# Attention tiles that are read back by mirror: transposes two steps ahead, fetches in one list

## The chip, the cores and the metric

The kernel runs on one core of a Trainium2 chip. The time is that of one execution on the device in microseconds (us), of the slowest core, which here is the only one. Shown is the median of 3 runs. TensorE (PE in the rows) multiplies matrices, PEld is its weight load; VectorE (DVE), ScalarE (ACT) and GpSimd (POOL) do the work on elements; SyncE (SP) issues nearly all transfers.

## The reference

Attention without softmax, then an MLP, in float32:

```python
B, S, D = u.shape                       # 4, 3008, 256
scores = (1.0 / S) * np.matmul(z, z.transpose(0, 2, 1))    # z: 4 x 3008 x 64
attn = np.maximum(scores, 0.0) ** 2
x = (u * np.matmul(attn, v)).reshape(B * S, D)
h = x @ w_in                            # 256 -> 2048
g = h * np.clip(h + 3.0, 0.0, 6.0) / 6.0
return (g @ w_out).astype(np.float32)   # 2048 -> 256
```

The scores are a product of z with itself, so the matrix `attn` of a batch is symmetric.

## The kernel before

**Tiles.** A batch has 6 chunks c of queries (five of 512, the last of 448) and 12 pairs p of key blocks (two blocks of 128 keys). One step of the main loop (L546 to L602) is one pair of one chunk, 288 steps in all, g = 12 i + p, with i the chunk's number over all batches. In a step TensorE adds the pair's product with v to two accumulators `o` (`av`, 12 matmuls), and beside it runs units of the MLP of an earlier chunk: `up` (matmuls into `h`) and `down` (matmuls into `y`), 16 units a chunk. Each float32 operand is split into a high and a low part: `ah` and `al` of the attention, `gh` and `gl` of the MLP, `xh` and `xl` of its input. So each product takes three matmuls.

**New and mirrored pairs.** `scores` (L289) prepares the pair that is used one step later (two steps later for the first 28). Where the key block p // 2 is not below c, the pair is new: TensorE computes `s`, ACT and DVE make `rt`, its square `r2`, `ah` and `al`, and `keep` (L242) writes the square to DRAM in tiles `d` if a later chunk needs it. Where p // 2 < c, the pair is the mirror image of one computed before, and `from_mirror` (L259) makes it: chunk c has 2c such pairs, 30 a batch, 120 in all. `fetch_mirrored` (L226) reads such a tile `l` from `d` with four DMAs on SyncE's queue (two buffers of `l`). DVE then transposes it in two instructions into `rm` (L272), ACT casts `rm` to `ah` (L275) and DVE subtracts, `al` (L277):

```python
nc.vector.transpose(out=to, in_=of)                 # L272, twice: rm <- l
nc.scalar.copy(out=ah[:, :, :n], in_=rn)            # L275
nc.vector.tensor_tensor(out=al[:, :, :n], in0=rn, in1=f(ah[:, :, :n]), op=ALU.subtract)
```

**The MLP's chain.** After `up`, ACT makes `rt` from `h` (L396), DVE multiplies it (`rt`, L397), and later (`late`, run by `flush`) ACT casts `gh` (L80) and DVE subtracts `gl` (L81). `down` uses them. After the last `up` of a chunk, `urgent` makes this split run ahead of the next pair's `ah`.

**The chunk border.** When pair 11 is done, DVE multiplies each accumulator by `u` (`times_u`, L366). There is one buffer for each of the two `o`, so the next chunk's first matmul waits for this.

**What sets the order.** The instructions are issued in the order in which the code calls them; each engine works through its own in that order. In a step the loop calls `scores` for the pair ahead (L559), then fetches for the pairs up to two beyond it (L562), then loads and weight work, then `attend` (`av`, and `times_u` at the border), then the MLP's units. The tiles `rt`, `r2`, `rm` and raw weights share five buffers (`rpool`), the `ah` and `gh` share four (`apool`), and so do the `al` and `gl`.

Of the kernel before, what the change touches and what calls it, by code (L numbers as in the profile page):

```python
# [9 lines left out]
F32R = mybir.dt.float32r  # L10
# [5 lines left out]
P = 128  # L16
CH = 512
# [13 lines left out]
def relu2_attention_then_hswish_mlp(  # L31
# [30 lines left out]
    apool = ctx.enter_context(tc.tile_pool(name="apool", bufs=4))  # L62
# [9 lines left out]
    def f(ap):  # L72
        return ap.bitcast(F32)
# [19 lines left out]
    def flush_copies():  # L93
        while copies:
            copies.pop(0)()
# [72 lines left out]
    def fetch_v(b, p):  # L168

        if b == 0 and p < NPAIR - 1:  # L170
            raw = vpool.tile([P, 2, D], F32, tag="vl", name="vraw")
        else:
            raw = stg.tile([P, 2, D], F32, tag="stg", name="vraw")
        vh = vpool.tile([P, 2, D], F32R, tag="vh", name="vh")
        vt[b, p] = vh
        raws["v", p] = raw
        j0 = p * 2 * P
        for dst, queue in ((raw, nc.sync), (vh, nc.gpsimd))[:1 if b else 2]:
            if p < NPAIR - 1:
                queue.dma_start(  # L180
                    out=dst, in_=v[b, j0:j0 + 2 * P, :].rearrange("(r q) d -> q r d", q=P)
                )
            else:
                queue.dma_start(out=dst[:, 0, :], in_=v[b, j0:j0 + P, :])
                for h in range(2):
                    queue.dma_start(out=dst[64 * h:64 * h + 64, 1, :], in_=v[b, j0 + P:S, :])
# [7 lines left out]
    def fetch_z(b, k):  # L194
        if b == 0:
            raw = xpool.tile([P, CH], F32, tag=("xh0", "xh1", "xl0", "xl1")[k % 4], name="zraw")
        else:
            raw = stg.tile([P, CH], F32, tag="stg", name="zraw")
        zx = zpool.tile([P, CH], F32R, tag="zx", name="zx")
        zy = zpool.tile([P, CH], F32R, tag="zy", name="zy")  # L200
        zt[b, k] = (zx, zy)
        raws["z", k] = raw
        cols = slice(k * CH, (k + 1) * CH)
        nc.sync.dma_start(out=raw, in_=zz[b, :, cols])
        if b == 0 and k > 1:
            nc.gpsimd.dma_start(out=zx[0:64], in_=zz[b, 0:64, cols])
            nc.gpsimd.dma_start(out=zy[64:128], in_=zz[b, 64:128, cols])
# [11 lines left out]
    def flush():  # L219
        urgent.clear()  # L220
        while late:
            late.pop(0)()

    kept, mirrored = {}, {}

    def fetch_mirrored(b, c, p):  # L226


        if p // 2 >= c:
            return  # L230
        src = kept[b, p // 2, c]
        nk = width(c) // 32
        t = lpool.tile([P, 16, 64], F32, tag="l", name="l")
        for q in range(4):
            c0 = q * P + (p % 2) * 64
            nc.sync.dma_start(  # L236
                out=t[32 * q:32 * q + 32, :nk, :],
                in_=src[:, c0:c0 + 64].rearrange("(k e) f -> e k f", e=32),
            )
        mirrored[b, c, p] = t  # L240

    def keep(b, c, p, r2):  # L242

        k = p // 2
        if k <= c:
            return
        if p % 2 == 0:
            kept[b, c, k] = dpool.tile([width(k), CH], F32, tag=f"d{c}{k}", name=f"d{c}{k}")
        dst = kept[b, c, k]
        j0 = (p % 2) * 2 * P  # L250
        if p < NPAIR - 1:
            nc.sync.dma_start(
                out=dst[j0:j0 + 2 * P].rearrange("(r q) n -> q r n", q=P), in_=r2
            )
        else:
            nc.sync.dma_start(out=dst[j0:j0 + P], in_=r2[:, 0])
            nc.sync.dma_start(out=dst[j0 + P:j0 + P + 64], in_=r2[0:64, 1])

    def from_mirror(b, c, p):  # L259
        n = width(c)  # L260
        t = mirrored.pop((b, c, p))
        rn = rpool.tile([P, 2, CH], F32, tag="r", name="rm")[:, :, :n]
        ah = apool.tile([P, 2, CH], F32R, tag="ah", name="ah")
        al = apool.tile([P, 2, CH], F32R, tag="al", name="al")
        for r in range(2):
            if c < NCH - 1:
                to = rn[:, r].rearrange("p (q j e) -> p j q e", q=4, j=4)
                of = t.rearrange("p (j q) (r e) -> p r j q e", q=4, r=2)[:, r]
            else:
                to = rn[:, r].rearrange("p (k e) -> p k e", e=32)  # L270
                of = t[:, :n // 32, 32 * r:32 * r + 32]
            nc.vector.transpose(out=to, in_=of)  # L272
        if urgent:
            flush()
        nc.scalar.copy(out=ah[:, :, :n], in_=rn)  # L275
        flush_copies()
        nc.vector.tensor_tensor(  # L277
            out=al[:, :, :n], in0=rn, in1=f(ah[:, :, :n]), op=ALU.subtract
        )
        at[b, c, p] = (ah, al)  # L280
        flush()
# [7 lines left out]
    def scores(b, c, p, square_on_act=False):  # L289


        if p // 2 < c:
            return from_mirror(b, c, p)
# [38 lines left out]
    def width(c):  # L332
        return CH if c < NCH - 1 else S - CH * (NCH - 1)
# [98 lines left out]
    pairs = [(b, c, p) for b, c in chunks for p in range(NPAIR)]  # L432
# [62 lines left out]
    def weight_work(n):  # L495
        for _ in range(n):
            next(w_ops, None)
# [31 lines left out]
    with tc.manual_schedule():  # L529
        nc.vector.memset(three, 3.0)  # L530
        fetch_z(0, 0)
        fetch_v(0, 0)
        split_z(0, 0)
        fetch_z(0, 1)
        fetch_v(0, 1)
        weight_work(1)
        split_v(0, 0)
        split_z(0, 1)
        scores(0, 0, 0)
        fetch_z(0, 2)  # L540
        fetch_v(0, 2)
        scores(0, 0, 1)
        fetch_v(0, 3)
        g_done = 2
        g_fetched = 2
        for i, (b, c) in enumerate(chunks):  # L546
            ahead = b + 1 if c == NCH - 1 and b + 1 < B else None
            for p in range(NPAIR):
                g = i * NPAIR + p
                lead = 2 if g < FIRST else 1  # L550
                if i == 0:
                    if p + 1 < NPAIR:
                        split_v(0, p + 1)
                    if p % 2 == 0 and p // 2 + 2 < NCH:
                        split_z(0, p // 2 + 2)
                early = lead == 2 and p == NPAIR - 1
                if early:
                    attend(b, c, p)
                while g_done < min(g + lead + 1, len(pairs)):  # L559
                    scores(*pairs[g_done], square_on_act=i < 3)  # L560
                    g_done += 1
                while g_fetched < min(g_done + 2, len(pairs)):  # L562
                    fetch_mirrored(*pairs[g_fetched])
                    g_fetched += 1
                if i == 0:
                    if p + 4 < NPAIR:
                        fetch_v(0, p + 4)
                    if p % 2 == 0 and p // 2 + 3 < NCH:
                        fetch_z(0, p // 2 + 3)
                    if p == 6:  # L570
                        load_u(*chunks[0])
                        load_u(*chunks[1])
                maybe_split()
                if g >= FIRST:
                    weight_work(5)
                elif p < NPAIR - 2:
                    weight_work(4 if i else 2)
                if ahead and p < NPAIR - 1:
                    if p:
                        split_v(ahead, p - 1)  # L580
                    if p < NPAIR - 2:
                        fetch_v(ahead, p)
                    if p % 2 == 1:
                        fetch_z(ahead, p // 2)
                    elif p:
                        split_z(ahead, p // 2 - 1)
                elif b and c == 0 and p < 4:
                    if p in (1, 2):
                        split_v(b, NPAIR - 3 + p)
                    if p < 2:  # L590
                        fetch_v(b, NPAIR - 2 + p)
                    if p == 2:
                        fetch_z(b, NCH - 1)
                    if p == 3:
                        split_z(b, NCH - 1)
                if not early:
                    attend(b, c, p)
                if p == NPAIR - 1:
                    avs[0] += 1
                total = len(pairs) - FIRST  # L600
                target = max(0, g + 1 - FIRST) * ((len(chunks) - 1) * NU - 4) // total
                mlp_units(target - units_done[0])  # L602
        mlp_units(1)
        maybe_split()
        mlp_units(len(chunks) * NU - units_done[0])
# [46 lines left out]
```

## Time and profile before

| | |
|---|---|
| median of 3 runs | 2040.76 us (2036.39 to 2044.0) |
| the profiled execution | 2040.08 us |
| its span, from the first to the last instruction | 2038.3 us |
| granted TensorE clock, mean | 0.994 of full speed |
| TensorE matmuls busy | 1982.9 us, 97% |
| TensorE weight loads busy | 1634.6 us, 80% |
| VectorE busy | 1290.6 us, 63% |
| ScalarE busy | 989.7 us, 49% |
| DMA, mean | 87 GB/s |

How to read it: the busy time of an engine is the sum of its instructions' rows, and idle time is what lies between them. A row in order of time has the start, the duration, engine, line, operation, output and inputs, and in brackets how long the engine had idled before it and what ended that idling. Matmuls are pipelined: a row of one overlaps that of the next. A weight load stands a matmul or so ahead of the matmul that uses it.

### The profile page before, as it was taken

How to read it: one execution, taken by the hardware profiler on the slowest of the kernel's cores; microseconds unless marked ns; L12 is line 12 of the kernel's file. 1: busy time of each engine (PE TensorE's matmuls, PEld its weight loads, DVE VectorE, ACT ScalarE, POOL GpSimd, SP SyncE). 2: the span in 40 equal slices, each digit the busy share in tenths (PEclk: the TensorE clock that was granted, in tenths of full speed). 3: DMA queues.
4: the chain of work that ended last, by engine and by line, in shares of the span. 5: the costliest groups of instructions: out<-in, count | busy, mean ns of one | idle time of the engine just before them, and what ended most of it. 6: DMA issues, size and time to landing. Idle time of an engine off the chain costs nothing.

```text
span 2038.3 us, 22016 instructions
## 1 busy us (share of the span) xinstructions
PE 1982.9 (97%) x8688; PEld 1634.6 (80%) x8688; DVE 1290.6 (63%) x1397; ACT 989.7 (49%) x1057; POOL 14.2 (1%) x26
## 2 busy tenths in 40 slices
PE   8989999999999999999999999999999999999999
PEld 6767787888888877888888888788888887778888
DVE  7888666676556566667555666566756565556654
ACT  7754444465444444445545444444654544444444
POOL 2000000000000000000000000000000000000000
PEclk9999999999999999999999999999999999999999
DMA  9644151512222414252123141424222323232400
GB/s 298 194 112 121 53 111 47 129 56 104 70 88 53 111 32 111 56 131 78 71 70 102 42 116 34 101 60 118 86 93 60 100 46 107 52 91 51 101 19 20
DMA packets 313351, 178.14 MB, mean 87 GB/s; under 512 B 248480, under 2 KB 265888, under 8 KB 313248
## 3 DMA queue, kind: packets, MB, share of 16 engines
q1 hardware_dynamic: 309312, 172.54, 31.8%
q0 software_dynamic: 3936, 4.20, 0.9%
q8 instruction: 68, 1.11, 0.2%
q14 instruction: 35, 0.29, 0.0%
HBM read 104.07 MB, written 72.61 MB: 87 GB/s over the span
## 4 chain that ended last, share of the span: by engine, by line
PE 75%; DVE 10%; ACT 6%; DMA 5%; issue 3%; SPq 1%; POOL 0%; DVEq 0%; ACTq 0%; POOLq 0%
PE o L76 29%; PE h L76 20%; PE y L76 20%; PE s L76 7%; DVE rm L272 3%; DMA l<-d 2%; DVE al L277 2%; ACT ah L275 2%; DVE rt L397 1%; ACT rt L396 1%; DVE gl L81 1%; ACT gh L80 1%; SPq L236 1%; DMA vraw<-in_v_dram 1%; DMA vh<-in_v_dram 1%
## 5 line engine op out<-in xcount | busy, mean ns | idle before, releaser
L397 DVE SCALAR_TENSOR_TENSOR rt<-rt,h 128x1024 f32<-128x1024 f32 (+1 forms) x192 | 230.0, 1198 | 407.8 <-ACT rt L396 407.7
L76 PE MATMUL o<-ah,vl 128*128 128x512 f32 (+1 forms) x1152 | 450.3, 391 | 26.0 <-DVE u L366 20.0
L76 PE MATMUL o<-ah,vh 128*128 128x512 f32 (+1 forms) x1152 | 450.5, 391 | 0.0
L76 PE MATMUL o<-al,vh 128*128 128x512 f32 (+1 forms) x1104 | 435.9, 395 | 11.5 <-DVE al L277 9.9
L396 ACT ACTIVATE rt<-h,three 128x1024 f32<-128x1024 f32 (+1 forms) x192 | 210.9, 1098 | 462.8 <-PE h L76 462.7
L76 PE MATMUL y<-gl,w_out_h 128*128 128x512 f32 (+1 forms) x768 | 297.1, 387 | 3.5 <-DVE gl L81 3.5
L76 PE MATMUL y<-gh,w_out_l 128*128 128x512 f32 (+1 forms) x768 | 297.0, 387 | 2.6 <-ACT gh L80 1.7
L76 PE MATMUL y<-gh,w_out_h 128*128 128x512 f32 (+1 forms) x768 | 296.4, 386 | 0.0
L76 PE MATMUL h<-xh,w_in_l 128*128 128x512 f32 (+1 forms) x768 | 296.2, 386 | 0.0
L76 PE MATMUL h<-xl,w_in_h 128*128 128x512 f32 (+1 forms) x768 | 296.0, 385 | 0.0
L76 PE MATMUL h<-xh,w_in_h 128*128 128x512 f32 (+1 forms) x768 | 295.9, 385 | 0.0
L76 PEld LDWEIGHTS o<-ah,vl 128*128 128x128 f32 x1152 | 218.6, 190 | 81.5 <-issue 26.5
L81 DVE TENSOR_TENSOR gl<-rt,gh 128x1024 fp32r<-128x1024 f32 (+1 forms) x192 | 230.2, 1199 | 68.5 <-ACT gh L80 67.8
L76 PEld LDWEIGHTS o<-al,vh 128*128 128x128 f32 x1104 | 209.6, 190 | 69.9 <-DVE al L277 25.5
L275 ACT CAST ah<-rm 128x1024 fp32r<-128x1024 f32 (+1 forms) x120 | 121.7, 1014 | 294.3 <-DVE rm L272 287.4
L76 PEld LDWEIGHTS o<-ah,vh 128*128 128x128 f32 x1152 | 218.3, 190 | 40.9
L80 ACT CAST gh<-rt 128x1024 fp32r<-128x1024 f32 (+1 forms) x192 | 197.1, 1026 | 102.2 <-DVE rt L397 102.2
L307 ACT ACTIVATE rt<-s 128x1024 f32<-128x1024 f32 x168 | 171.2, 1019 | 114.3 <-PE s L76 110.7
L313 DVE TENSOR_TENSOR r<-rt 128x1024 f32<-128x1024 f32 (+1 forms) x140 | 170.0, 1214 | 87.7 <-ACT rt L307 87.5
L277 DVE TENSOR_TENSOR al<-rm,ah 128x1024 fp32r<-128x1024 f32 (+1 forms) x120 | 141.7, 1181 | 126.8 <-ACT ah L275 126.7
L76 PEld LDWEIGHTS y<-gl,w_out_h 128*128 128x128 f32 x768 | 144.5, 188 | 31.8 <-DVE gl L81 5.1
L76 PEld LDWEIGHTS y<-gh,w_out_l 128*128 128x128 f32 x768 | 144.5, 188 | 31.7 <-ACT gh L80 3.3
(52 smaller groups left out, 1867.7 us busy)
## 6 DMA issues: line engine op xcount, KB each, us to landing
l<-d SPq DMA_DIRECT2D x320, 128.0 KB, 3.4
d<-r SPq DMA_DIRECT2D x79, 512.0 KB, 2.8
l<-d SPq DMA_DIRECT2D x160, 112.0 KB, 2.9
vraw<-in_v_dram SPq DMA_DIRECT2D x44, 256.0 KB, 3.3
d<-rt SPq DMA_DIRECT2D x21, 512.0 KB, 3.2
u<-in_ut_dram SPq DMA_DIRECT2D x20, 512.0 KB, 4.2
out_dram<-y SPq DMA_DIRECT2D x40, 256.0 KB, 3.2
zraw<-in_zz_dram SPq DMA_DIRECT2D x24, 256.0 KB, 3.6
```

What stands on the lines that cost most here:

```text
L76: nc.tensor.matmul(out, lhsT=lhsT, rhs=rhs, start=start, stop=stop)
L80: nc.scalar.copy(out=hi, in_=raw)
L81: nc.vector.tensor_tensor(out=lo, in0=raw, in1=f(hi), op=ALU.subtract)
L236: nc.sync.dma_start(out=t[32 * q:32 * q + 32, :nk, :], in_=src[:, c0:c0 + 64].rearrange("(k e) f -> e k f", e=32),)
L272: nc.vector.transpose(out=to, in_=of)
L275: nc.scalar.copy(out=ah[:, :, :n], in_=rn)
L277: nc.vector.tensor_tensor(out=al[:, :, :n], in0=rn, in1=f(ah[:, :, :n]), op=ALU.subtract)
L307: nc.scalar.activation(out=rn, in_=s[:, :, :n], func=AF.Relu, scale=1.0 / S)
L313: nc.vector.tensor_tensor(out=r2, in0=rn, in1=rn, op=ALU.mult)
L396: nc.scalar.activation(out=rn, in_=h, func=AF.Relu, bias=three)
L397: nc.vector.scalar_tensor_tensor(out=rn, in0=rn, scalar=6.0, in1=h, op0=ALU.min, op1=ALU.mult)
```

## The change

The function `from_mirror` is cut in two. `turn` does the transposes and is called in its own loop, one pair ahead of `scores`: at step g of the later part of the program the pair g + 2 is transposed, where before it was pair g + 1. `from_mirror` keeps the cast and the subtraction. The fetches no longer follow the list of all pairs: `to_fetch` lists mirrored pairs alone, in their order over all chunks and batches, and the next one is fetched as soon as fewer than two fetched tiles stand untransposed and its tile in DRAM is complete (`whole`). This is tried behind each `turn` and in each step with p > 3.

```diff
-    kept, mirrored = {}, {}
-
-    def fetch_mirrored(b, c, p):
-        if p // 2 >= c:
-            return
+    kept, mirrored, turned, whole = {}, {}, {}, set()
+    to_fetch = []
+
+    def fetch_mirrored():
+        while to_fetch and len(mirrored) < 2:
+            b, c, p = to_fetch[0]
+            if (b, p // 2, c) not in whole:
+                return
+            fetch_pair(*to_fetch.pop(0))
+
+    def fetch_pair(b, c, p):
         src = kept[b, p // 2, c]
...
+        if p % 2 == 1:
+            whole.add((b, c, k))
-    def from_mirror(b, c, p):
+    def turn(b, c, p):
+        if p // 2 >= c:
+            return
         n = width(c)
         t = mirrored.pop((b, c, p))
         rn = rpool.tile([P, 2, CH], F32, tag="r", name="rm")[:, :, :n]
-        ah = apool.tile([P, 2, CH], F32R, tag="ah", name="ah")
-        al = apool.tile([P, 2, CH], F32R, tag="al", name="al")
...
             nc.vector.transpose(out=to, in_=of)
+        turned[b, c, p] = rn
+        fetch_mirrored()
+
+    def from_mirror(b, c, p):
+        n = width(c)
+        rn = turned.pop((b, c, p))
+        ah = apool.tile([P, 2, CH], F32R, tag="ah", name="ah")
+        al = apool.tile([P, 2, CH], F32R, tag="al", name="al")
...
-        g_fetched = 2
+        to_fetch += [(b, c, p) for b, c, p in pairs if p // 2 < c]
+        g_turned = 2
...
-                while g_fetched < min(g_done + 2, len(pairs)):
-                    fetch_mirrored(*pairs[g_fetched])
-                    g_fetched += 1
+                if p > 3:
+                    fetch_mirrored()
+                while g_turned < min(g_done + 1, len(pairs)):
+                    turn(*pairs[g_turned])
+                    g_turned += 1
```

The instructions of TensorE, ACT and GpSimd stand in the order of before. On DVE the transposes move. First a stretch within chunk 2 of batch 3 (it ran at 1645 to 1659 us), two MLP units and two mirrored pairs; before:

```order
L397 SCALAR_TENSOR_TENSOR rt<-rt,h 128x1024
L272 STREAM_TRANSPOSE rm<-l 128x4x4x32 x2
L277 TENSOR_TENSOR al<-rm,ah 128x1024
L81 TENSOR_TENSOR gl<-rt,gh 128x1024
L397 SCALAR_TENSOR_TENSOR rt<-rt,h 128x1024
L272 STREAM_TRANSPOSE rm<-l 128x4x4x32 x2
L277 TENSOR_TENSOR al<-rm,ah 128x1024
L81 TENSOR_TENSOR gl<-rt,gh 128x1024
```

and the same place of the changed kernel, on DVE:

```order
L415 SCALAR_TENSOR_TENSOR rt<-rt,h 128x1024
L295 TENSOR_TENSOR al<-rm,ah 128x1024
L81 TENSOR_TENSOR gl<-rt,gh 128x1024
L282 STREAM_TRANSPOSE rm<-l 128x4x4x32 x2
L415 SCALAR_TENSOR_TENSOR rt<-rt,h 128x1024
L295 TENSOR_TENSOR al<-rm,ah 128x1024
L81 TENSOR_TENSOR gl<-rt,gh 128x1024
L282 STREAM_TRANSPOSE rm<-l 128x4x4x32 x2
```

The transposes of a pair have moved from between `rt` and `al` to a place ahead of `rt`, behind the `al` of the pair before.

Then the border between chunks 3 and 4 of batch 2 (1292 to 1308 us), on DVE, from the last `gl` ahead of it; before:

```order
L81 TENSOR_TENSOR gl<-rt,gh 128x1024
L397 SCALAR_TENSOR_TENSOR rt<-rt,h 128x1024
L272 STREAM_TRANSPOSE rm<-l 128x4x4x32 x2
L277 TENSOR_TENSOR al<-rm,ah 128x1024
L81 TENSOR_TENSOR gl<-rt,gh 128x1024
L366 TENSOR_TENSOR u<-u,o_8919 128x512
L366 TENSOR_TENSOR u<-u,o_8926 128x512
L272 STREAM_TRANSPOSE rm<-l 128x4x4x32 x2
L277 TENSOR_TENSOR al<-rm,ah 128x1024
```

and the same border of the changed kernel, on DVE:

```order
L81 TENSOR_TENSOR gl<-rt,gh 128x1024
L282 STREAM_TRANSPOSE rm<-l 128x4x4x32 x2
L415 SCALAR_TENSOR_TENSOR rt<-rt,h 128x1024
L295 TENSOR_TENSOR al<-rm,ah 128x1024
L81 TENSOR_TENSOR gl<-rt,gh 128x1024
L282 STREAM_TRANSPOSE rm<-l 128x4x4x32 x2
L384 TENSOR_TENSOR u<-u,o_8927 128x512
L384 TENSOR_TENSOR u<-u,o_8934 128x512
L295 TENSOR_TENSOR al<-rm,ah 128x1024
```

The first pair's transposes now stand ahead of `rt`, and the second pair's ahead of the two `u` instead of behind them.

Last, SyncE's queue in chunk 0 of batch 0 (it issued these from 33 to 40 us); before:

```order
L252 DMA d_340<-rt 128x2x512
L180 DMA vraw<-in_v_dram 128x2x256
L204 DMA zraw<-in_zz_dram 128x512
L252 DMA d_340<-rt 128x2x512
L180 DMA vraw<-in_v_dram 128x2x256
```

and the same place of the changed kernel, on SyncE:

```order
L259 DMA d_340<-rt 128x2x512
L243 DMA l<-d_183 32x16x64 x8
L180 DMA vraw<-in_v_dram 128x2x256
L204 DMA zraw<-in_zz_dram 128x512
L259 DMA d_340<-rt 128x2x512
L180 DMA vraw<-in_v_dram 128x2x256
```

The eight fetches of the first two mirrored tiles, which stood behind the last stores of the chunk, now stand ahead of a `vraw` and a `zraw` in its middle.

## Rows read from the trace of the kernel before

**Rows 1.** The page: busy time of the engines, share, instructions.

```profile
PE 1982.9 (97%) x8688; PEld 1634.6 (80%) x8688; DVE 1290.6 (63%) x1397; ACT 989.7 (49%) x1057; POOL 14.2 (1%) x26
```

**Rows 2.** Busy time by stretch: length, then each engine's, with its instructions.

```profile
1450.00:1550.00 100.00, 100.00 (x450) 84.17 (x449) 63.92 (x64) 54.65 (x60) 0.00 (x0) 1.00 0.25 77
```

**Rows 3.** Who waited for whom: total us, times, longest; TensorE's matmuls.

```profile
PE o L76 <- DVE u L366: 20.0, 11, 4.5
```

**Rows 4.** The same view, TensorE's weight loads.

```profile
PEld o L76 <- DVE al L277: 25.5, 39, 1.1
...
PEld o L76 <- ACT ah L275: 5.6, 7, 1.4
PEld y L76 <- DVE gl L81: 5.1, 5, 1.3
...
PEld y L76 <- ACT gh L80: 3.3, 4, 1.0
```

**Rows 5.** The same view, VectorE's wait ahead of `rt`.

```profile
DVE rt L397 <- ACT rt L396: 407.7, 157, 6.4
```

**Rows 6.** In order of time, VectorE, within chunk 2 of batch 3.

```profile
1652.70 1.22 DVE L397 SCALAR_TENSOR_TENSOR rt<-rt,h 128x1024 f32<-128x1024 f32 x1 [2.31 <-ACT rt L396]
1653.84 1.30 DVE L272 STREAM_TRANSPOSE rm<-l 128x512 f32<-128x512 f32 x2
1656.32 1.23 DVE L277 TENSOR_TENSOR al<-rm,ah 128x1024 fp32r<-128x1024 f32 x1 [1.18 <-ACT ah L275]
```

**Rows 7.** The same stretch, ScalarE.

```profile
1655.23 1.05 ACT L275 CAST ah<-rm 128x1024 fp32r<-128x1024 f32 x1 [2.56 <-DVE rm L272]
```

**Rows 8.** The same stretch, matmuls and weight loads.

```profile
1656.73 0.39 PE L76 MATMUL o<-ah,vl 128*128 128x512 f32 x1
...
1657.59 0.19 PEld L76 LDWEIGHTS o<-al,vh 128*128 128x128 f32 x1 [0.90 <-DVE al L277]
1657.60 0.50 PE L76 MATMUL o<-al,vh 128*128 128x512 f32 x1 [0.47 <-DVE al L277]
...
1657.93 0.39 PE L76 MATMUL o<-ah,vh 128*128 128x512 f32 x1
```

**Rows 9.** In order of time, ScalarE, behind a chunk's last up-projection.

```profile
370.10 1.05 ACT L80 CAST gh<-rt 128x1024 fp32r<-128x1024 f32 x1 [1.29 <-DVE rt L397]
371.19 0.95 ACT L275 CAST ah<-rm 128x896 fp32r<-128x896 f32 x1
```

**Rows 10.** In order of time, VectorE, at the border to chunk 4, batch 2.

```profile
1298.25 1.22 DVE L397 SCALAR_TENSOR_TENSOR rt<-rt,h 128x1024 f32<-128x1024 f32 x1 [4.01 <-ACT rt L396]
...
1301.80 1.22 DVE L277 TENSOR_TENSOR al<-rm,ah 128x1024 fp32r<-128x1024 f32 x1 [1.12 <-ACT ah L275]
1302.94 1.22 DVE L81 TENSOR_TENSOR gl<-rt,gh 128x1024 fp32r<-128x1024 f32 x1
1304.08 1.28 DVE L366 TENSOR_TENSOR u<-u,o 128x512 f32<-128x512 f32 x2
```

**Rows 11.** The same, at the border to chunk 3, batch 1.

```profile
703.34 1.28 DVE L366 TENSOR_TENSOR u<-u,o 128x512 f32<-128x512 f32 x2
```

**Rows 12.** Busy time by stretch, as rows 2; behind POOL's, TensorE's granted clock.

```profile
386.00:389.60 3.60, 2.01 (x9) 1.25 (x8) 2.60 (x3) 3.06 (x4) 0.00 (x0) 1.00 0.42 95
389.70:393.00 3.30, 3.30 (x10) 2.82 (x9) 2.85 (x5) 0.68 (x2) 0.00 (x0) 0.50 0.59 185
...
1045.00:1048.20 3.20, 3.20 (x9) 2.72 (x9) 2.20 (x3) 0.94 (x1) 0.00 (x0) 0.50 0.00 0
```

**Rows 13.** In order of time, matmuls, at the first border.

```profile
63.31 0.47 PE L76 MATMUL o<-ah,vl 128*128 128x512 f32 x1 [2.29 <-DVE u L366]
```

**Rows 14.** In order of time, SyncE and VectorE at the start: issue and use of one `zraw`.

```profile
34.14 1.06 SPq L204 DMA_DIRECT2D zraw<-in_zz_dram  x1
...
42.26 0.68 DVE L81 TENSOR_TENSOR zy<-zraw,zx 64x512 fp32r<-64x512 f32 x1
```

**Rows 15.** The fetched tile `l`: from issue to landing.

```profile
DMA to landing us min/median/max: 2.1/3.2/6.7
```

## The prediction

> **What bounds the kernel now.** I read the page's engine line first: TensorE (PE) shows matmuls for 1982.9 us of 2038.3, while VectorE (DVE) and ScalarE (ACT) are busy 63% and 49% [rows 1]. TensorE sets the end, and the question is what it loses between matmuls. The second view is the table of stretches: from 1450 to 1550 us, where no wait stands, 450 matmuls take 100 us, 0.222 us each [rows 2]. All 8688 at that pace are 1931 us, so some 107 us of the span are start, end, stalls and slow clock.
>
> The idle time in the engine line, 55.4 us, shows less than that, because a matmul's row is 0.39 us long though the next one starts after 0.23 [rows 8]. The Trainium skill (Perfetto Trace Analysis, Identifying the Most-Contended Engine) says that matmul busy time is a poor measure and the busy share of the weight loads a good one. The trace agrees: loads are 84.17% of the unbroken stretch and 80% of the whole, and 1634.6 / 0.8417 is 1942 us, 96 below the span. By the busy share, no change here could win over 55 us; by the loads, up to 96.
>
> The third view is who waits. TensorE's matmuls waited 20.0 us in 11 places for DVE's `u`, the product that empties the accumulators `o` at a chunk border [rows 3]. Its weight loads (PEld) waited 25.5 us in 39 places for `al`, 5.6 in 7 for `ah`, 5.1 in 5 for `gl` and 3.3 in 4 for `gh` [rows 4]. The last view is time order around one such wait. At 1652.70 DVE does `rt` of the MLP, which it awaited for 2.31 us; then the two transposes, 1.30 us; ACT casts `ah` at 1655.23 after idling 2.56 us for them; DVE, idle 1.18 us, makes `al` from 1656.32 [rows 6, 7]; TensorE needed it at 1656.96 and got it at 1657.60 [rows 8]. So transpose, cast and subtraction run in a chain behind an instruction that itself waits for TensorE, and DVE idles in front of that instruction 407.7 us in 157 waits, 2.6 us in each [rows 5].
>
> **The change, part by part.** The orders of TensorE, ACT and GpSimd stay as they were, and no instruction is added or removed. Moved are DVE's 120 pairs of transposes and SyncE's 480 fetches.
>
> *Transposes one step earlier, within a chunk.* The pair (1.30 us) now stands ahead of `rt`, in the 2.3 us which DVE idled there [rows 6], and the cast needs nothing from `rt`, so ACT does it right behind its own part of `rt`. At 1653.9, where the transposes began, DVE can start `al` at once: 2.4 us earlier, against a wait of 0.90. What is late next is `gl`, made behind `al`; it comes 2.4 us earlier too, since in the old order it stood behind the same chain. So I count all waits of rows 4 as gone: 25.5 + 5.6 + 5.1 + 3.3 = 39.5 us in 55 places. A load runs up to one matmul ahead, so TensorE loses less than the load waits: in the sample three starts lie 0.87 and 0.33 us apart instead of 0.23 each [rows 8], a loss of 0.75 for a wait of 0.90. With 0.15 off for each, 39.5 becomes 31.2 us. In three places the wait stays. They follow the last up-projection of a chunk, where `gh` and `gl` are made ahead of `ah` and `al`: at 370.10 `gh` waits 1.29 us for `rt` and `ah` comes behind it on ACT, whenever the transpose was done [rows 9]. By the gaps between matmuls there these three are 0.8, 0.7 and 1.6 us, 3.1 together. **Gain: 31.2 - 3.1 = 28.1 us.** From both sides: the cover was 2.3 us for 1.3 in the sample, so I do not expect a loss; if the transposes delayed `rt` wherever cover is short, half of it could go (a rival below). Above, nothing more than 31.2 is there.
>
> *At chunk borders.* There the following tile's transposes now stand ahead of the two `u`. With 0.16 us hidden under each matmul row (0.39 less 0.23), the 11 waits are 21.8 us. At 1298.25 the old order is `rt`, transposes, idle 1.12 us, `al`, `gl`, `u` at 1304.08 [rows 10]. The new one is `rt`, `al`, `gl`, the next transposes, `u`: 1299.4 + 1.2 + 1.2 + 1.3 = 1303.1. The idle of 1.12 goes, the transposes are only exchanged for others: 0.9 us of 2.85 won. Five borders are of this kind (0.85 to 1.0 each: 4.7 us). Three with a wait under 0.5 us lose it whole (1.1). The first one, which ended at 63.31 [rows 13], wins 0.9 by the same count. But at the border whose `u` ran at 703.34 [rows 11], `gl` waits for `gh` behind `rt`, and the old transposes lay in that wait; the new ones stand between `al` and the `xl` in front of `u`, which slips to 704.6: 1.3 us lost. Four more borders lose 0.25 to 0.35 in the same way (1.15 together). **Gain: 4.7 + 1.1 + 0.9 - 1.3 - 1.15 = 4.2 us.** Some 17 us of border waits stay. Bounds: -5 (all borders like the one at 703) to +21.8.
>
> *The clock.* From 386 us, where TensorE stalls for an `ah` and its `al`, 9 matmuls start in 3.6 us; in the 3.3 us behind it the granted clock is half, 1.2 GHz, and 10 start instead of 15. The same stands behind a stall for `gh` and `gl` at 1045 [rows 12]. The first part removes both stalls, and each of the two stretches costs half its 3.4 us. **Gain: 3.4 us.** Half clock stands also behind the long border waits, the one of [rows 10] among them, which stay; I leave it there. Bounds: 0 to 6.8, if two of those go too.
>
> *Fetches.* They are as many, and each is still issued two tiles ahead of its transposes, behind the transposes that free its buffer. Across a chunk border they are earlier. Only the first eight move into the busy start: they stand ahead of a `vraw` and the `zraw` whose issue ran at 34.14. Eight issues of about 0.5 us put it at 38.1, and DVE uses that `zraw` at 42.26 [rows 14], 4 us later, with TensorE's need behind that. The landing of fetches ranges from 2.1 to 6.7 us [rows 15]. So I bound the cost by 0 and 3 us and take 0, since DVE's cast of it is used only some 4 us later.
>
> **Sum.** 28.1 + 4.2 + 3.4 = 35.7 us. The profiled execution took 2040.08 us around its span of 2038.3; less 35.7 it is 2004.4. The median of the runs shown is 0.7 higher, which gives 2005; I forecast 2004, between both.
>
> **The rivals.**
> 1. *The room ahead of `rt` is too short.* The transposes then push `rt`, `gh` and `gl`, and TensorE waits for these instead. For it: 2.6 us is a mean, and 35 of the 192 `rt` show no wait at all. Against it: the mean is twice the 1.3 needed, and the old place stood behind `rt` but ahead of `gl`. At half the first part and no border gain: 2040 - 14 - 3.4 = 2023.
> 2. *The borders go too.* If DVE, relieved within the chunk, arrives at each border early, the remaining 17 us and two more slow stretches go: 2004 - 17 - 3.4 = 1984. Against it: at 1298.25 `rt` is tied to TensorE's own product, not to DVE's lateness [rows 10].
> 3. *Slower: the transposes hold DVE for their fetch.* They stand a step nearer to the fetch's landing, and all behind them, `rt` and `u` included, would wait. The price decides from the point where a fetch lands later than the two steps (some 14 us, at 288 steps in 2034 us) plus the 2.6 us of cover. Issues of 2 us and the longest landing of 6.7 make 8.7 [rows 15], so 5 us are spare. Were each of 120 tiles 0.8 us beyond the cover, 96 us would come on top: 2004 + 96 = 2100; at half the tiles 2052. The Trainium skill (TensorE: Matmul & The Clock Gate, opening table) calls the queues of ScalarE and VectorE strict first-in-first-out, which is the rule behind this rival; the trace shows DVE in that order, but hardly a wait for a fetch.
> 4. *The change does not do what it says.* The tiles of the transposes come from the same five buffers as `rt` and `r2`; if these came free only when they did, the transposes would run when they ran: 2040. Against it: five allocations reach back two steps or more.
>
> **How the numbers follow.** Forecast 0.65, rival 1 0.15, rival 2 0.08, rival 3 0.05, rival 4 0.07. The range is 1990 to 2026: it takes in rival 1 and the bounds of clock and start (2004 - 3.4 - 10 at the borders; 2004 + 3 + half the first part). About 0.5%, 10 us, is what a measurement of this kernel can tell from no change. Forecast and rivals 1 and 2 are faster by more: 0.88, of which I give 0.01 away for rival 1 near its slow end, 0.87; rival 4 and a little is the same, 0.08; rival 3 slower, 0.05.
>
> **What would show it.** Right: the loads' waits for `al` fall from 25.5 us to under 5, those for `gl` and `gh` to under 2; ACT's idle for the transposes (2.56 in the sample) is gone, DVE's idle before `rt` shrinks by about 1.3 us; the waits for `u` stay at 14 to 20 us, and the one near 703 grows to 1.5 us or more; no half clock at 390 and 1045. Wrong: DVE waiting for fetches, `rt` starting later behind ACT than now, a wait at the start for `zraw`, or the waits for `al` of the same size.

## The result and the profile after

The changed kernel takes 2009.2 us (median; 2005.3 to 2011.0) against 2040.4 us (2036.4 to 2044.0): a ratio of 0.9845, 95% interval 0.9821 to 0.9869, 31 us faster. The forecast was 2004, the range 1990 to 2026. The sum was nearly met, its terms less so: the start, which I had put at nothing, cost 4 to 8 us, and the stretches within the chunks gave 3 less than counted, while the borders and the clock behind the first two chunks gave more. That these errors in part cancel is luck.

The engine line of the changed kernel's page, the answer to [rows 1]:

```profile
PE 1967.8 (98%) x8688; PEld 1636.7 (81%) x8688; DVE 1288.2 (64%) x1397; ACT 989.2 (49%) x1057; POOL 14.2 (1%) x26
```

The work is the same to 0.2% on every engine but PE, so what went is waiting and slow clock. The span fell by 29.1 us to 2009.2, the idle time of PE's row only from 55.4 to 41.4. By the loads (81% of the span, 84.44% of an undisturbed stretch, the first row below) the distance of the span from an undisturbed one fell from 96 to 71 us, which is 25 of the 29. The reading that the Trainium skill advises (Perfetto Trace Analysis, Identifying the Most-Contended Engine) proved the better one in this pair of traces too.

Stretches of the changed kernel, columns as in [rows 2], the second to last but one being TensorE's clock. The second and third lie behind the places that [rows 12] show:

```profile
1430.00:1530.00 100.00, 100.00 (x451) 84.44 (x450) 63.88 (x64) 53.59 (x59) 0.00 (x0) 1.00 0.29 85
...
390.40:393.70 3.30, 3.30 (x17) 2.84 (x16) 3.30 (x6) 1.74 (x2) 0.00 (x0) 1.00 0.16 36
1033.00:1036.20 3.20, 3.20 (x17) 2.68 (x16) 2.19 (x3) 1.79 (x2) 0.00 (x0) 1.00 0.79 164
50.90:57.70 6.80, 4.92 (x12) 3.89 (x13) 6.70 (x11) 3.00 (x3) 0.00 (x0) 0.50 1.04 373
```

At both places the granted clock is now full and 17 matmuls start instead of 10 or 9. But near the start there is a half-clock stretch of 6.8 us that the kernel before did not have, and over the first 125 us the mean granted clock fell from 0.97 to 0.92.

The waits of the changed kernel: total us, times, longest (answers to [rows 3 to 5]):

```profile
PE o L76 <- DVE u L384: 11.9, 7, 3.6
...
PEld o L76 <- DVE al L295: 4.8, 5, 1.3
PEld o L76 <- ACT ah L293: 4.7, 3, 2.7
...
PEld y L76 <- DVE gl L81: 2.4, 4, 1.1
...
DVE rt L415 <- ACT rt L414: 429.6, 164, 6.4
...
ACT ah L293 <- DVE rm L282: 75.6, 30, 3.6
...
DVE al L295 <- ACT ah L293: 33.0, 26, 2.4
```

The loads' waits for `al` fell from 25.5 us to 4.8, `gh` left the list, and those for `ah` fell from 7 to 3 (4.7 us, of which 2.7 at 66.7 us, a new one at the start, and 1.5 at 388). ScalarE's idle time for the transposes went from 287.4 us to 75.6 (sixth row). What the prediction did not see is the fifth row: VectorE's idle time ahead of `rt` did not shrink, it grew by 22 us. The idle ahead of `al` shrank by 94 us; in the kernel before that row was

```profile
DVE al L277 <- ACT ah L275: 126.7, 111, 2.1
```

and a share of it collected ahead of `rt`, where VectorE in the end waits for TensorE's `h`. Here is the sample of [rows 6 to 8] in the changed kernel, 21 us earlier. VectorE:

```profile
1631.36 1.22 DVE L415 SCALAR_TENSOR_TENSOR rt<-rt,h 128x1024 f32<-128x1024 f32 x1 [4.03 <-ACT rt L414]
1632.50 1.22 DVE L295 TENSOR_TENSOR al<-rm,ah 128x1024 fp32r<-128x1024 f32 x1
1633.70 1.23 DVE L81 TENSOR_TENSOR gl<-rt,gh 128x1024 fp32r<-128x1024 f32 x1
1634.85 1.30 DVE L282 STREAM_TRANSPOSE rm<-l 128x512 f32<-128x512 f32 x2
```

and TensorE, where that pair's product begins:

```profile
1635.45 0.39 PE L76 MATMUL o<-ah,vl 128*128 128x512 f32 x1
1635.68 0.39 PE L76 MATMUL o<-al,vh 128*128 128x512 f32 x1
1635.90 0.39 PE L76 MATMUL o<-ah,vh 128*128 128x512 f32 x1
```

`al` begins right behind `rt`, 1.14 us after it instead of 3.62, and the three matmuls start 0.23 apart: the wait of 0.90 is gone. VectorE's two waits of 2.31 and 1.18 us have become one of 4.03.

To see what each stretch gave I took, from both traces, the distance between every two matmul starts less the undisturbed one of its shape (0.227 us for 512 columns), and added up what is over (us):

| | before | after | gain | forecast |
|---|---|---|---|---|
| attention within a chunk, from chunk 2 of batch 0 on | 34.9 | 14.6 | 20.3 | |
| MLP's `y`, from there on | 10.2 | 5.5 | 4.7 | 28.1 with the row above |
| first matmul of a chunk (border), from there on | 20.8 | 15.4 | 5.4 | 3.3 |
| half clock, from there on | 9.2 | 3.0 | 6.2 | 3.4 |
| all of chunks 0 and 1 of batch 0 | 14.5 | 22.6 | -8.1 | 0.9 |
| the rest | | | 0.3 | |
| sum | | | 28.8 | 35.7 |

Of the forecast's 4.2 us for the borders, 0.9 belong to the first one (at 63.31), so they stand in the row of chunks 0 and 1.

The place of the 8.1 us, on SyncE and VectorE of the changed kernel (the answer to [rows 14]):

```profile
35.18 7.41 SPq L243 DMA_DIRECT2D l<-d  x8
42.63 0.49 SPq L180 DMA_DIRECT2D vraw<-in_v_dram  x1
43.17 0.47 SPq L204 DMA_DIRECT2D zraw<-in_zz_dram  x1
...
48.04 0.68 DVE L81 TENSOR_TENSOR zy<-zraw,zx 64x512 fp32r<-64x512 f32 x1 [5.11 <-DMA zraw<-in_zz_dram]
```

and TensorE, its matmuls with an idle time between 46 and 69 us:

```profile
49.54 0.48 PE L76 MATMUL s<-zy,zx 128*128 128x512 f32 x1 [2.59 <-issue]
52.78 0.76 PE L76 MATMUL o<-ah,vl 128*128 128x512 f32 x1 [2.05 <-DVE vl L81]
66.76 0.47 PE L76 MATMUL o<-ah,vl 128*128 128x512 f32 x1 [2.31 <-DVE vl L81]
```

The eight fetches took 7.41 us to issue, so `zraw` went out 9 us later than before and VectorE, idle 5.11 us for it, used it 5.8 us later. Three stalls follow (2.75, 2.2 and 2.47 us over the undisturbed distance), and half clock from 50.9 us on. Of the 8.1 us about 5 are longer stalls and 4 are half clock, less 1 in small gaps. The third stall stands before the product for which the kernel before waits 1.18 us; the 1.3 us between them are as long as the transposes (1.30) that now stand ahead of that `vl`. The stall of 2.46 us at the first border, right behind, is gone. The same start lost 18.9 us in the profile of run 4 below, which issues the same instructions there but shows no first stall, so the cost against the kernel before is put at 4 to 8 us, from one profile of each.

### The profile page after: what moved, and what is told of

The parts are those of the page before. It is cut to its first block, busy times and chain, and to the rows that moved or that the text cites. A ratio compares the mean times of both kernels' runs of the same rounds, so it can differ in the third digit from the quotient of the medians.

```text
span 2009.2 us, 22027 instructions
## 1 busy us (share of the span) xinstructions
PE 1967.8 (98%) x8688; PEld 1636.7 (81%) x8688; DVE 1288.2 (64%) x1397; ACT 989.2 (49%) x1057; POOL 14.2 (1%) x26
## 4 chain that ended last, share of the span: by engine, by line
PE 88%; DVE 5%; DMA 2%; ACT 2%; issue 1%; SPq 1%; DVEq 0%; ACTq 0%; POOLq 0%
PE o L76 34%; PE h L76 24%; PE y L76 23%; PE s L76 7%; DVE rm L282 1%; DVE rt L415 1%; DMA zraw<-in_zz_dram 1%; DMA vraw<-in_v_dram 1%; DVE al L295 1%; ACT rt L414 1%; ACT gh L80 1%; DVE gl L81 0%; SPq L243 0%; DMA l<-d 0%; ACT rt L325 0%
## 5 line engine op out<-in xcount | busy, mean ns | idle before, releaser
L76 PE MATMUL o<-ah,vl 128*128 128x512 f32 (+1 forms) x1152 | 449.3, 390 | 21.1 <-DVE u L384 11.9
L76 PEld LDWEIGHTS y<-gl,w_out_h 128*128 128x128 f32 x768 | 144.3, 188 | 29.1 <-DVE gl L81 2.4
L76 PEld LDWEIGHTS y<-gh,w_out_l 128*128 128x128 f32 x768 | 144.3, 188 | 29.1 <-DVE w_out_l L136 1.3
L76 PEld LDWEIGHTS h<-xh,w_in_h 128*128 128x128 f32 x768 | 144.3, 188 | 27.0
L76 PEld LDWEIGHTS h<-xh,w_in_l 128*128 128x128 f32 x768 | 144.3, 188 | 27.0 <-DVE rt L415 0.2
```

What stands on the lines that cost most here:

```text
L76: nc.tensor.matmul(out, lhsT=lhsT, rhs=rhs, start=start, stop=stop)
```

## The experiments

Every time below is a median, every ratio is to the kernel before with its 95% interval; the changed kernel itself is at 2009.2. The kernel before, timed again beside each group of runs, took 2041.5 us (runs 1 to 4), 2040.0 (5 to 8) and 2038.7 (9), so medians of different groups compare to 1 to 3 us only.

**1. First fetches as late as before.** 

```diff
-                if p > 3:
+                if p > 3 and (i or p > 7):
                     fetch_mirrored()
```

> The changed kernel, but the first fetches wait until step 8 of chunk 0, as late as before; all else is as in the changed kernel. Theory (the changed kernel loses 7.7 us in its first 250 us because eight fetches stand ahead of a vraw and the zraw on SyncE's queue: zraw issued at 43.17 instead of 34.14): zraw is issued by 36 us again, the stalls of TensorE at 46.6 (2.75 us) and 50.3 (2.2 us) shrink by at least 3 us together, the half clock from 50.9 to 57.7 goes, and the time is 2001 to 2004, 5 to 8 us under the 2009.2 of the changed kernel. Rival A (those stalls belong to the transposes, which at the start stand ahead of the casts of v and z on VectorE): the fetches' place changes nothing, 2008 to 2010. Rival B (a fetch issued late is then what a transpose waits for): VectorE shows waits for a DMA into l, and the time is over 2010.

Measured: 2009.2 us, 0.9843 (0.9828 to 0.9858). In time the theory missed and rival A was met (2008 to 2010); in the trace the theory held up to 54 us, against rival A. `zraw` was issued at 35.04, both stalls are gone, and pair 10 of chunk 0 starts 0.75 us later than in the kernel before instead of 8.0. Then what rival B describes took over. VectorE and TensorE of this run:

```profile
59.86 1.30 DVE L282 STREAM_TRANSPOSE rm<-l 128x512 f32<-128x512 f32 x2 [3.54 <-DMA l<-d]
...
62.12 0.69 DVE L81 TENSOR_TENSOR vl<-vraw,vh 128x512 fp32r<-128x512 f32 x1
```

```profile
62.95 0.76 PE L76 MATMUL o<-ah,vl 128*128 128x512 f32 x1 [5.64 <-DVE vl L81]
```

The first transpose, moved a step forward, waits 3.54 us for its fetch, and the `vl` behind it is late for TensorE, which stalls where it loses 1.2 us in the kernel before. Of the 8.1 us at the start 5.1 remain. The 3 us won were lost again as half clock, 6.8 us of it near 386 us, behind a stall of 2.7 us, longer than the changed kernel's 1.24. In both kernels ScalarE waits ahead of the stall to cast `vraw` to `vh`. Here `vraw` was issued at 373.13 and the cast began 6.8 us later, against 4.0 in the changed kernel (its rows stand at run 5). So the extra length came from a slower landing, not from a later issue; why it landed slower is not shown.

**2. Early transposes, old list of fetches.** `fetch_mirrored` is emptied. Behind the loop of `turn` stands the old list, reaching one pair further than before, as the transposes do:

```diff
+                while g_fetched < min(g_done + 3, len(pairs)):
+                    fetch_pair(*pairs[g_fetched])
+                    g_fetched += 1
```

> Half of the change: transposes two steps ahead of use, but the fetches by the old list of all pairs, which ends at a chunk border until the step count reaches the next mirrored pair. Theory (the gain comes from the early transposes alone, and the single list only costs at the start and in the stall at 386.7 us, where fetches stand ahead of vraw and zraw): 1999 to 2003, waits of the loads for al under 6 us. Rival (the single list is needed: without it the transposes wait for their fetch behind each border): VectorE shows waits for l, some 1 us or more at each of the borders to a chunk with mirrored pairs, and the time is 2012 or more.

Measured: 2005.7 us, 0.9829 (0.9816 to 0.9842), between the two marks and nearer to the theory's; the waits for `al` are 6.4 us, just above the 6 expected. VectorE's and the loads' waits:

```profile
DVE rm L280 <- DMA l<-d: 2.6, 2, 1.8
```

```profile
PEld o L76 <- DVE al L293: 6.4, 6, 1.3
```

The two waits for a fetch are those of the first two mirrored tiles, at 58.81 and 63.67; no later pair of transposes waits for one. So the early transposes alone bring the whole gain, and the single list adds nothing to it. The start loses 2.8 us here. That the old list is better by 3.5 us than the new one is likely from the traces (the start), but the two intervals overlap.

**3. The new list, old transposes.** `turn` is called at the head of `from_mirror`, and its own loop is taken out:

```diff
     def from_mirror(b, c, p):
+        turn(b, c, p)
         n = width(c)
```

> The other half of the change: the fetches in the one list of mirrored pairs, over chunk borders, with the transposes at their old place between rt and al. Theory (the list alone gains nothing in the steady part and costs at the start): the loads' waits for al are as in the kernel before (25 us, and 5 or so each for ah and gl), half clock stands at 390 and 1045 us again, and the time is 2043 to 2049, 3 to 8 us above the kernel before. Rival (the list gains something over borders, where a fetch was late): 2036 or less, with the waits for u shorter.

Measured: 2043.6 us, 1.0016 (1.0005 to 1.0027), at the theory's lower mark. The loads' waits and two half-clock stretches of this run:

```profile
PEld o L76 <- DVE al L296: 25.9, 38, 1.1
PEld o L76 <- ACT ah L294: 7.9, 8, 3.1
PEld y L76 <- DVE gl L81: 5.1, 5, 1.3
```

```profile
395.10:398.30 3.20, 3.20 (x9) 2.85 (x10) 3.20 (x4) 1.27 (x2) 0.00 (x0) 0.50 0.94 240
1050.50:1053.70 3.20, 3.20 (x10) 2.85 (x9) 2.19 (x3) 0.94 (x1) 0.00 (x0) 0.50 0.02 1
```

All waits of the kernel before are back, and the half clock at the same two places, 5.5 us later, since the start costs 5.3. But not all of its half clock: at the borders to chunk 4 of batch 2 and chunk 3 of batch 3 TensorE loses 3.02 us in both kernels, yet only in the kernel before half clock follows. Behind the first of the two, the kernel before and this run:

```profile
1304.40:1307.70 3.30, 2.79 (x7) 2.25 (x8) 2.17 (x4) 1.02 (x1) 0.00 (x0) 0.50 0.04 6
...
1311.20:1314.60 3.40, 3.40 (x16) 2.80 (x17) 2.21 (x4) 1.05 (x1) 0.00 (x0) 1.00 0.17 40
```

**4. Transposes behind `u` at the border.** 

```diff
-                while g_turned < min(g_done + 1, len(pairs)):
+                border = p == NPAIR - 1 and not early
+                while g_turned < min(g_done + 1, len(pairs)) and not border:
                     turn(*pairs[g_turned])
...
                     attend(b, c, p)
+                while g_turned < min(g_done + 1, len(pairs)):
+                    turn(*pairs[g_turned])
+                    g_turned += 1
```

> The changed kernel, but in the last pair of a chunk of the later part the next tile's transposes come behind the two u instead of ahead of them. Theory (the u that empties the accumulators is up to 1.3 us late because a pair of transposes stands right ahead of it on VectorE, as at 1287.11 ahead of the u of 1288.33): the stalls of TensorE at the borders near 701, 784, 1201, 1287, 1621, 1708 and 1794 us (1.48, 0.51, 1.38, 1.86, 0.62, 1.86 and 0.27 us) lose most of their size, 6 to 7 us together, and the time is 2001 to 2004. Rival A (the u is late because rt, gl and xl ahead of it are tied to TensorE's own product): the stalls keep over two thirds of their size, 2007 to 2010. Rival B (the transposes behind u now delay the next chunk's al or rt): new waits for al behind each border as long as what the u gained, 2008 to 2012.

Measured: 2001.4 us, 0.9810 (0.9797 to 0.9824), the theory's lower mark, 7.8 us under the changed kernel. First the border to chunk 4 of batch 2 in the changed kernel, the answer to [rows 10]:

```profile
1284.76 1.22 DVE L295 TENSOR_TENSOR al<-rm,ah 128x1024 fp32r<-128x1024 f32 x1
...
1287.11 1.30 DVE L282 STREAM_TRANSPOSE rm<-l 128x512 f32<-128x512 f32 x2
1288.33 1.25 DVE L384 TENSOR_TENSOR u<-u,o 128x512 f32<-128x512 f32 x2
```

and the same border in this run:

```profile
1276.55 1.22 DVE L295 TENSOR_TENSOR al<-rm,ah 128x1024 fp32r<-128x1024 f32 x1
...
1278.90 1.28 DVE L384 TENSOR_TENSOR u<-u,o 128x512 f32<-128x512 f32 x2
1280.09 1.30 DVE L282 STREAM_TRANSPOSE rm<-l 128x512 f32<-128x512 f32 x2
```

TensorE's loss at this border is 3.02 us in the kernel before, 1.86 in the changed one, 0.68 here. Over all borders from chunk 2 on it fell from 15.4 to 7.7 us, about the 7.8 between the medians. Attention within the chunks lost as much as in the changed kernel (14.7 against 14.6), so almost nothing was given back behind the border.

**5. Fetches behind the step's loads.** 

```diff
-                if p > 3:
-                    fetch_mirrored()
...
+                if i or p > 7:
+                    fetch_mirrored()
                 if not early:
                     attend(b, c, p)
```

with the call in `turn` taken out.

> The changed kernel, but in each step the fetches are issued behind that step's loads of v, z and u instead of ahead of them, and the first ones not before step 8 of chunk 0. Theory (loads queued behind fetches on SyncE's queue are late for ScalarE, as at 382.71, where vh and the zx cast waited for vraw and zraw and held rt and ah: stalls of 1.24 and 1.23 us in the changed kernel, 2.71 and 1.23 with the first fetches late): the stalls near 383 us shrink under 0.7 us together, no half clock follows there, the start is as with the first fetches late (o of chunk 1 about 5 us later than in the kernel before), and the time is 2001 to 2005. Rival (a fetch issued behind the loads lands too late for its transposes): VectorE waits for l in the steady part, 2009 or more.

Measured: 2003.4 us, 0.9821 (0.9808 to 0.9835), the theory's time. ScalarE and SyncE of the changed kernel near 383 us:

```profile
374.99 3.15 SPq L243 DMA_DIRECT2D l<-d  x4
...
378.71 0.47 SPq L180 DMA_DIRECT2D vraw<-in_v_dram  x1
```

```profile
382.71 0.62 ACT L80 CAST vh<-vraw 128x512 fp32r<-128x512 f32 x1 [6.70 <-DMA vraw<-in_v_dram]
```

and ScalarE of this run:

```profile
376.61 0.62 ACT L80 CAST vh<-vraw 128x512 fp32r<-128x512 f32 x1 [5.38 <-DMA vraw<-in_v_dram]
```

Chunk 5 as a whole starts 4.8 us earlier here, this cast 6.1. With the loads ahead of the four fetches (3.15 us) the stalls behind it (1.24 and 1.23) became 0.44 and 1.23: the first shrank, the second, expected to shrink too, did not. Its length is the time by which `al` comes behind `ah`: VectorE does the MLP's `rt` in between (387.36 to 388.58 in the changed kernel, `al` from 388.49), here too, so an earlier load moves both. No half clock followed, and none in the steady part after 191 us. VectorE waits for `l` there once, 2.19 us at 783.36. Against run 1, which has the first fetches as late, TensorE loses 7 us less in this profile, 4 of them half clock.

**6. Both edits together** (4 and 5).

> Fetches behind the loads (as in the run before) and the transposes behind u at chunk borders (the border edit that took 7.8 us off) together. Theory (the two are independent): 1993 to 1998. Rival (the border edit's gain and the loads' order share one cause, since both relieve the same stretch of VectorE at a batch's last chunk): 1999 or more.

Measured: 1997.8 us, 0.9791 (0.9778 to 0.9805), at the upper end of the theory's span. The border's losses are those of run 4 (7.7 us). But the later fetches begin to be waited for; VectorE of this run:

```profile
619.37 1.31 DVE L282 STREAM_TRANSPOSE rm<-l 128x512 f32<-128x512 f32 x2 [4.58 <-DMA l<-d]
```

It is followed by a stall of TensorE's `y` of 1.03 us at 622.9; another wait, of 1.66 us, stands at 780.88. So the edits are not quite independent, and a fetch behind the loads has little room left.

**7. The transposes done twice.** 

```diff
-            nc.vector.transpose(out=to, in_=of)
+            for _ in range(2):
+                nc.vector.transpose(out=to, in_=of)
```

> The changed kernel with every pair of transposes executed twice over, 1.3 us more VectorE work for each of 120 tiles. Theory (ahead of rt VectorE idles 2.6 us on average and the room holds 1.3 us and most of 2.6): only the borders, where the second pair stands ahead of u too, lose about 1.3 us each in 7 to 10 places, and some places within the chunks: 2018 to 2030, waits for al under 15 us. Rival (the first of the prediction's: the room was just enough or too short): each further 1.3 us shows at half of the tiles or more, 2060 or more, rt on VectorE later and waits of the loads for gl and gh back at 5 us or more each.

Measured: 2072.7 us, 1.0160 (1.0140 to 1.0180). The time is that of the rival, the marks (waits for `al` under 15 us, for `gl` and `gh` under 5) are the theory's:

```profile
PE o L76 <- DVE u L385: 43.5, 16, 6.6
...
PEld o L76 <- DVE al L296: 9.5, 9, 1.4
```

Those for `gl` and `gh` are 3.7 and 2.6 us.

VectorE had 162 us more to do (1450.7 against 1288.2) and TensorE lost 63. Of that 34 us lie at the borders (15.4 to 49.1) and 18 in the half clock that followed them (3.0 to 20.6); attention within the chunks lost 7 and the MLP's `y` 5. I had counted 1.3 us at 7 to 10 borders. VectorE at the border to chunk 3 of batch 2 shows why it is more:

```profile
1237.25 2.79 DVE L283 STREAM_TRANSPOSE rm<-l 128x512 f32<-128x512 f32 x4
1241.21 1.23 DVE L296 TENSOR_TENSOR al<-rm,ah 128x1024 fp32r<-128x1024 f32 x1 [1.18 <-ACT ah L294]
1242.35 2.79 DVE L283 STREAM_TRANSPOSE rm<-l 128x512 f32<-128x512 f32 x4
1245.07 1.25 DVE L385 TENSOR_TENSOR u<-u,o 128x512 f32<-128x512 f32 x2
```

Two doubled pairs stand in the chain that ends with `u`, each 1.49 us longer (2.79 against 1.30), and the loss at this border grew by 2.98 us. Four other borders grew by as much and five by 1.5, that of one pair. In all the loss grew by 0.9 to 3.0 us, at 17 borders.

**8. As 6, with the first two tiles transposed at their old place.** 

```diff
     def from_mirror(b, c, p):
+        if (b, c, p) not in turned:
+            turn(b, c, p)
...
+                if i == 0:
+                    border, g_turned = True, g_done
```

and the loop of `turn` behind `attend` begins with chunk 1.

> As the run with both edits, and in chunk 0 of batch 0 the transposes of the first two mirrored tiles at their old place, one step later. Theory (with the first fetches late, the first transpose waits for its fetch on VectorE, 56.32 to 59.86 us, and holds the vl behind it: a stall of TensorE of 5.8 us before pair 11 of chunk 0, where the kernel before has 1.2): that stall is 1.2 to 1.5 us again, chunk 1 of batch 0 starts within 1.5 us of the kernel before, and the time is 1988 to 1993. Rival (the vl of the last keys is late by itself): the stall stays over 4 us, 1993 to 1998.

Measured: 1995.8 us, 0.9782 (0.9769 to 0.9795). The stall before pair 11 is 1.14 us, and chunk 1 of batch 0 starts 1.5 us after that of the kernel before, as the theory said. But the time, only 2 us under run 6, is the rival's, since the stall moved on to the border behind it. TensorE of this run:

```profile
58.57 0.47 PE L76 MATMUL o<-ah,vl 128*128 128x512 f32 x1 [0.98 <-DVE vl L81]
64.81 0.47 PE L76 MATMUL o<-ah,vl 128*128 128x512 f32 x1 [2.78 <-DVE u L385]
```

The transposes still wait for the fetch (2.00 us), now between that `vl` and `u`. This is the lowest median, 13 us under the changed kernel; run 6 can't be told from it.

**9. Twice, and behind `u` at the border** (7 and 4).

> Every pair of transposes executed twice, as in the run that took 2072.7 us, and in the last pair of a chunk of the later part the transposes behind u, as in the run that took 2001.4. Theory (the 63 us that the doubled transposes cost are lost at chunk borders, 34 us in longer waits for u and some 18 in the half clock that follows them, and not in the room ahead of rt): with one of the two pairs ahead of u gone, the border stalls shrink by 2.6 us each and most of the half clock goes: 2025 to 2045; the loads' waits for al, gl and gh stay at 10, 4 and 3 us. Rival (VectorE is short within the chunks too, and the border is only where this comes out): what the border gains is lost in the next steps, 2055 or more, with longer waits for al, gl and gh.

Measured: 2037.4 us, 0.9994 (0.9984 to 1.0003), 35 us under run 7: the border losses fell from 49.1 to 16.3 us, the half clock from 20.6 to 11.6, attention within the chunks stayed at 21 (21.7 and 21.3), while the MLP's `y` rose by 6. The loads' waits for `al`, `gl` and `gh` are 11.0, 5.0 and 4.3 us, each 1 to 2 above run 7. So more than half of the 63 us that run 7 costs was lost at the border. Not all: to run 4 it is still 36 us, of which the border and half clock are 19, the MLP's `y` 10 and attention 7. The room ahead of `rt` holds one pair of transposes, and a second one in most places, not in all.

## Why the prediction was right, and where it was not

**Within a chunk: right, a little large.** Counted 28.1 us, won 25.0. The chain stood behind `rt` as read from [rows 6 to 8], runs 2 and 3 show that moving the transposes alone removes it, and runs 7 and 9 that one pair had room there, since a second one for each of the 120 tiles costs no more than 12 to 17 us there (attention 7, `y` 5 to 10). The places that were to stay stayed: the losses at 373.1, 1895.2 and 212.3 us are 0.60, 0.66 and 1.22, 2.5 together (3.1 counted). What failed is "I count all waits of rows 4 as gone": at 386 us TensorE lost 2.0 us before and still loses 2.5, first for an `ah` that is late by the loads behind fetches on SyncE's queue (run 5 took 0.8 off it), then for the `al` behind the MLP's `rt`.

**Borders: right in kind, 3.3 counted from chunk 2 on, 5.4 won.** Five won 1.1 to 1.2 each, where 0.85 to 1.0 was counted. The border at 703 lost 1.1 us (0.37 to 1.48), 1.3 predicted. Two that I had counted, if at all, at a loss of 0.35 lost 1.2 and 0.6 (those at 1201 and 1621 us of the changed kernel). That the transposes ahead of `u` are the price is shown by run 4.

**The clock: inside the bounds, but only in part for the reason given.** I took 3.4 us and left half clock standing behind the borders that stay. All four stretches of the steady part went, near the upper bound of 6.8; the borders' stalls of 1.86 us are followed by none. But the two behind the borders are missing in run 3 as well, where TensorE waits there as long as before, so they can't be put down to the transposes. At 390 "The first part removes both stalls" failed: the stall stayed, and the half clock went all the same, to come back in run 1. Only at 1045 did stall and half clock go together, and both are back in run 3. So one stretch of the four, 1.7 us, is shown to be the change's, and the rest is luck as far as the runs tell. And the start gained half clock: over the whole span it fell only from 24 to 20 us, worth 1.7 us.

**The start: the failed step.** "Eight issues of about 0.5 us put it at 38.1 ... I bound the cost by 0 and 3 us and take 0": they took 7.41 us, `zraw` was issued at 43.17, and the loss in these two profiles is 8.1 us, outside the bound. The bound was taken from issues in the steady part and from one consumer, `zy`. The trace of the kernel before had a nearer price, for the same eight fetches at their old place:

```profile
50.93 3.95 SPq L236 DMA_DIRECT2D l<-d  x4
...
56.99 2.24 SPq L236 DMA_DIRECT2D l<-d  x4
```

That is 6.2 us instead of 4. The bound also left out the `vraw` behind the same fetches, the transposes that now stand ahead of the last `vl`, and the half clock that follows such stalls. Run 1 separates the two halves of this: with the fetches late the first half goes, and rival 3 (VectorE held by a transpose that waits for its fetch) appears in its place, for one tile, 3.54 us. The rule behind it, that these engines take their queues strictly in order (the Trainium skill, TensorE: Matmul & The Clock Gate, opening table), is what this trace shows: `vl` stood behind the transpose, and in run 8, with the transposes behind it, it began at 57.74 instead of 62.12.

**The rivals.** Rival 1 (room too short) fell: waits for `gl` and `gh` went down. Rival 2 (the borders go too) did not happen by itself, though the two slow stretches that it counted did go; run 4 took half of the border waits that were left. Rival 3 did not occur in the changed kernel (VectorE shows no wait for `l`). It came up in the runs that fetch later: at the start of 1, 2, 5, 6 and 8, and near 620 or 780 us in 5, 6 and 8. Rival 4 fell: in the sample the transposes run at 1634.85, ahead of the next `rt`.

**The signs.** `al` under 5 us (4.8), no half clock at 390 and 1045 (at 390 with a stall still there), ScalarE's idle for the transposes gone in the sample: right. `gh` under 2: right; `gl` 2.4, just not. `u` at 14 to 20 us: 11.9, and the border near 703 at 1.48 us, a little under the 1.5. VectorE's idle before `rt` shrinking by 1.3: wrong, since the idle of the removed waits came together there. "A wait at the start for `zraw`", named as a sign against me, stood there.

## What to carry to other kernels

An instruction that needs nothing from the one it stands behind belongs ahead of that engine's longest wait; then look at once at the place where it now stands ahead of something urgent (here `u` at the border, 7.8 us).
A transfer that is issued earlier has to be counted on the queue that issues it: every load behind it moves by its issue time, and where the queue is busy that is not the steady one (7.41 us for eight at the start; 3.15 and 1.95 for four near 375 and 380 us).
Price the start by itself. Its stalls have other causes than the steady part, and a wait moved there goes to the next instruction that is late (runs 1 and 8).

## What the runs showed of the hardware

A stall alone did not decide the clock. At the same place near 386 us, two stalls of 1.09 and 0.93 us (before) and of 2.71 and 1.23 (run 1) were followed by half clock, 1.24 and 1.23 (changed kernel) and 1.12 and 1.23 (run 2) were not. At borders a loss of 1.86 us was followed by none; one of 3.02 was in the kernel before and was not in run 3; one of 2.98 at the border to chunk 3 of batch 0 was in runs 1 and 5 and was not in the changed kernel and run 2. What else decides stays open.

Identical instructions at the start lost 22.6 us in one profile and 18.9 in another, with a whole kernel's runs spread over 6 us. The 37 executions of the kernel before beside runs 1 to 9 took 2036.4 to 2043.9 us, at a mean granted clock of 0.991 to 0.997. A term of that size, such as the start's or the clock's, can't be read from a single pair of traces.
